# An mLSTM cell followed by a multiplicative FFN: first feed-forward pieces of one 128-token block each, with sums, copies and row transfers moved between engines

## The chip, the core and the metric

The kernel runs on one core of a Trainium2 chip. A core has TensorE (PE: matmuls; its weight loads are shown apart as PEld), VectorE (DVE), ScalarE (ACT) and GpSimd (POOL), and SyncE (SP), which here only issues DMAs; a few more are issued from ScalarE's queue. Each engine works through its own queue in order. The metric is the device time of one execution in microseconds (us), lower is better.

## The reference

Four batches (B), eight heads (H), 768 positions (S), head dimension 40 (D). The first half is a recurrence with a matrix state; its output is the input of a feed-forward network without nonlinearity:

```python
for t in range(S):
    m_new = maximum(f[:, :, t] + m, i[:, :, t])
    f_stab, i_stab = exp(f[:, :, t] + m - m_new), exp(i[:, :, t] - m_new)
    C = f_stab * C + i_stab * outer(v_t, k_t);   n = f_stab * n + i_stab * k_t;   m = m_new
    y[:, :, t] = sigmoid(o_t) * (C @ q_t) / maximum(abs(n . q_t), 1.0)
x = y.transpose(0, 2, 1, 3).reshape(B * S, H * D)          # 3072 x 320
a, b = x @ w1, x @ w2                                      # 320 x 1024 each
out = ((a * b) @ w3) @ w_out                               # w3 1024 x 1024, w_out 1024 x 320
```

All inputs and the output are float32.

## The kernel before

**Blocks and steps.** The sequence is cut into blocks of 128 tokens of one batch: `NU = 24` blocks, block n being part n // 4 of batch n % 4. Four blocks form a group of 512 tokens (`gr`) for the feed-forward part. The main loop runs over 32 steps `s`; step s computes the scores and states of block s, the outputs of block s-1, and some feed-forward work on earlier blocks. The order on TensorE is the order of the program text. For the other engines too, the text's order is kept (`keep_order`), so an instruction that waits holds up all that stand behind it on its engine. PSUM outside the cell's own banks is a pool of four banks (`ps_m`); pt, px, pa, pb, wp are tiles of it.

**The cell.** For each block k, q, v and the output gate o are loaded (`load`, `load_o`), k and q are turned so that head dimensions lie on partitions, by TensorE and ScalarE (`turn`, tile pt) for blocks below 10 (`N_DVE`). From block 10 on `load_turned` brings them with eight DMAs in 32-row strips and VectorE transposes them (L317); the second strip of each pair is shifted by 32 columns. `weights` takes exponentials on ScalarE (L303, tile pw), `masks` zeroes the upper triangle on GpSimd (L308). Scores (ss) and state updates (pc) go to the PSUM tile `cell[0]`, a block's own products (ph) and the earlier state's (pi) to `cell[1]` (`quarter_work`; for blocks 0 and 1 ph is a tile of its own). `outputs` makes h = pi * g + ph on VectorE: one product (L423) and four sums of a quarter each (L430). Its steps then take the absolute value of the normaliser (L438), the maximum (L440), the reciprocal (L441), multiply it with the gate (L443) and give y (L445). The column of ones behind v, set by a memset, is what yields the normaliser.

**Turning y.** For blocks below 15 (`NY`), `x_trans` turns y on TensorE (tile px) and ScalarE copies it to xT (L486); `twice` copies the last 64 columns a second time on GpSimd (L476). From block 15 on, `send` writes y to DRAM with four DMAs (L456, L458), `get_back` reads it with four (L465) and `x_turn` transposes on VectorE (L472).

**Weights.** The matrices are fetched as pairs of 32-bit words, piece by piece, in the order of the list `todo`: ten pieces of w1 and w2 (`w12`: first the five of columns 0 to 511, then the five of columns 512 to 1023; the last of each five is the remainder `wr`), eight of w_out (`wo`), sixteen of w3. `fetch` issues the DMA; `scale_next` scales both words on ScalarE (L191, L195); `convert` shifts one (L199) and adds the other (L200) on VectorE, which gives a float32 piece; pieces of w3 are also transposed there (L248). `n_cvt[s]` says how many pieces are converted at the end of step s, and `n_fetch` and `converted + 4` how far the fetches run ahead. w3 @ w_out is formed once (`w3_mm`, tile wp, kept as w3o), from step 9 on.

**Feed-forward.** `up(gr, fs, cs)` multiplies w1 and w2 columns of the groups `fs` (128 columns each) with the tokens `cs` (tiles pa, pb), `up_rest` adds the last 64 rows (`wr`, four quarters of the array at a time), copies pa on ScalarE (L638) and multiplies with pb on VectorE (L639, tile ab). The list `ups` holds pieces of two column groups for 256 tokens; steps 2 to 5 take one each, steps 6 to 15 two. From step 16 on follow the output products (`ffn_out`) and, for the last three groups, a scheme with seven products instead of eight (`up_by_seven`, `out_by_seven`).

**Around step 2.** `quarter_work(2)` computes the outputs of block 1 and then calls `between`, which turns y of blocks 0 and 1, converts weight pieces, and starts the first piece of `ups` for tokens 0 to 255. Between the two turns it runs filler on TensorE whose result nobody reads: `warm(1, small=38)`, one 128x512 product and 38 of 64x64.

## Time and profile before

| | |
|---|---|
| median of 3 runs | 427.33 us (426.63 to 430.44) |
| span of the profiled execution | 425.8 us; the page names no other time for this execution |
| busy: PE, DVE, POOL, ACT | 414.1, 313.5, 154.3, 150.1 us |
| mean granted TensorE clock | 0.996 |
| DMA | 51.15 MB, 135211 packets, 109360 of them under 512 B |

How to read it: busy time is the time in which an engine had an instruction in work; the ends of matmuls are modelled, so a busy TensorE isn't one at its peak. A float32 matmul shows as two records. "Lxx" is a line of the kernel; most matmuls are recorded on one helper line, L92, and are told apart by their tiles. In the chain of waits each row has its start in the span, its length, and the engine and tile; "SPq" is a DMA being issued on SyncE's queue, "issue" is time for which the profile shows no cause. In groups of instructions the columns are output and inputs, shapes, count, busy us and mean ns, and the idle time just before them.

### The profile page before, as it was taken

How to read it: one execution, taken by the hardware profiler on the slowest of the kernel's cores; microseconds unless marked ns; L12 is line 12 of the kernel's file. 1: busy time of each engine (PE TensorE's matmuls, PEld its weight loads, DVE VectorE, ACT ScalarE, POOL GpSimd, SP SyncE). 2: the span in 40 equal slices, each digit the busy share in tenths (PEclk: the TensorE clock that was granted, in tenths of full speed). 3: DMA queues.
4: the chain of work that ended last, by engine and by line, in shares of the span. 5: the costliest groups of instructions: out<-in, count | busy, mean ns of one | idle time of the engine just before them, and what ended most of it. 6: DMA issues, size and time to landing. Idle time of an engine off the chain costs nothing.

```text
span 425.8 us, 13079 instructions
## 1 busy us (share of the span) xinstructions
PE 414.1 (97%) x5353; PEld 335.3 (79%) x5353; DVE 313.5 (74%) x635; ACT 150.1 (35%) x404; POOL 154.3 (36%) x211
## 2 busy tenths in 40 slices
PE   7989989999999999999999999999999999999996
PEld 4768878888688788787777778788778879888896
DVE  6676986888949779778736966596868699575971
ACT  4766865567723623630433313032311110210000
POOL 4421342233303303303307751546453587542100
PEclk9989999999999999999999999999999999999999
DMA  8999998598977776985425675756421120000001
GB/s 186 204 173 245 214 144 140 134 193 180 215 183 154 166 182 135 181 164 105 89 80 130 153 141 121 142 133 117 87 44 36 35 39 2 31 2 31 2 32 62
DMA packets 135211, 51.15 MB, mean 120 GB/s; under 512 B 109360, under 2 KB 126960, under 8 KB 135152
## 3 DMA queue, kind: packets, MB, share of 16 engines
q1 hardware_dynamic: 131552, 46.29, 53.9%
q10 hardware_dynamic: 3600, 4.03, 2.7%
q8 instruction: 42, 0.69, 0.7%
q14 instruction: 17, 0.14, 0.1%
HBM read 44.50 MB, written 5.80 MB: 118 GB/s over the span
## 4 chain that ended last, share of the span: by engine, by line
PE 53%; issue 20%; DVE 7%; POOL 7%; SPq 7%; DMA 5%; ACT 1%; POOLq 0%; DVEq 0%
PE cell L92 17%; PE pa L92 12%; PE o L92 8%; PE pb L92 8%; PE p L92 3%; POOL pw L308 3%; SPq L184 3%; DVE w3T L666 2%; PE pt L95 1%; POOL vw L330 1%; SPq L148 1%; DMA raw<-in_moe_w_dram 1%; PE fill L92 1%; POOL raw L659 1%; POOL state L335 1%
## 5 line engine op out<-in xcount | busy, mean ns | idle before, releaser
L335 POOL TENSOR_TENSOR state<-state,decay 128x164 f32<-128x164 f32 x40 | 20.0, 500 | 154.8 <-DVE state L404 129.0
L92 PE MATMUL pa<-xT,w 128*128 128x256 f32 x240 | 60.4, 382 | 0.0
L92 PEld LDWEIGHTS pa<-xT,w 128*128 128x128 f32 x240 | 44.4, 190 | 6.8 <-DVE h L430 0.4
L303 ACT ACTIVATE pw<-pw,aT 128x64 f32<-128x64 f32 x184 | 46.4, 339 | 3.2 <-ACT o_sb L741 1.9
L92 PE MATMUL pb<-xT,w 128*128 128x256 f32 x192 | 45.4, 379 | 0.0
L729 POOL TENSOR_TENSOR ab<-ab,a_sb 128x512 f32<-128x512 f32 x22 | 29.4, 1356 | 32.2 <-DVE ab L684 32.2
L92 PEld LDWEIGHTS pb<-xT,w 128*128 128x128 f32 x192 | 36.4, 190 | 5.0
L711 POOL TENSOR_TENSOR wo<-wo 128x512 f32<-128x512 f32 x22 | 27.4, 1268 | 29.8 <-DVE wo L686 29.8
L92 PE MATMUL pa<-xT,wr 64*64 64x256 f32 x384 | 37.0, 386 | 0.5 <-DVE wr L200 0.5
L92 PE MATMUL wp<-wo,w3T 128*128 128x320 f32 x128 | 35.9, 433 | 1.1 <-DVE ab L639 0.6
L308 POOL TENSOR_SCALAR_AFFINE_SELECT pw<-pw 64x512 f32<-64x512 f32 x48 | 35.8, 746 | 3.0 <-ACT pw L303 1.2
L92 PE MATMUL pb<-xT,wr 64*64 64x256 f32 x384 | 36.4, 380 | 0.0
L92 PE MATMUL cell<-w3o,ab 128*128 128x320 f32 x128 | 35.4, 432 | 0.0
L638 ACT ACTIVATE a_sb<-pa 128x512 f32<-128x512 f32 x24 | 14.3, 598 | 59.0 <-PE pb L92 59.0
L639 DVE TENSOR_TENSOR ab<-pb,a_sb 128x512 f32<-128x512 f32 x24 | 16.4, 688 | 23.2 <-ACT a_sb L638 22.8
L92 PEld LDWEIGHTS wp<-wo,w3T 128*128 128x128 f32 x128 | 23.8, 190 | 10.5 <-DVE ab L639 0.8
L92 PEld LDWEIGHTS cell<-w3o,ab 128*128 128x128 f32 x128 | 24.3, 190 | 9.5
L92 PEld LDWEIGHTS pa<-xT,wr 64*64 64x64 f32 x384 | 18.9, 132 | 15.4 <-issue 8.8
L686 DVE SCALAR_TENSOR_TENSOR a_sb<-pa,wo 128x512 f32<-128x512 f32 x12 | 8.3, 689 | 29.8 <-PE pa L92 29.8
L430 DVE TENSOR_TENSOR h<-cell,h 64x164 f32<-64x164 f32 x88 | 28.6, 326 | 1.6
L92 PE MATMUL po<-w3o,ab 128*128 128x320 f32 x96 | 26.4, 433 | 0.0
L92 PEld LDWEIGHTS po<-w3o,ab 128*128 128x128 f32 x96 | 18.1, 190 | 7.3
(180 smaller groups left out, 846.4 us busy)
## 6 DMA issues: line engine op xcount, KB each, us to landing
raw<-in_moe_w_dram SPq DMA_DIRECT2D x64, 128.0 KB, 3.4
kbuf<-in_k_dram SPq DMA_DIRECT2D x24, 160.0 KB, 4.5
v_all<-in_v_dram SPq DMA_DIRECT2D x24, 160.0 KB, 4.9
o_in<-in_o_gate_dram SPq DMA_DIRECT2D x24, 160.0 KB, 4.8
pw<-U_d SPq DMA_DIRECT2D x28, 128.0 KB, 3.5
raw<-in_moe_w_dram SPq DMA_DIRECT2D x5, 512.0 KB, 6.7
raw<-in_moe_w_out_dram SPq DMA_DIRECT2D x8, 320.0 KB, 4.1
gates<-in_k_dram SPq DMA_DIRECT2D x28, 80.0 KB, 2.5
```

The costliest lines, as they stand in the source:

```text
L92: in_order(nc.tensor.matmul(out, lhsT=lhsT, rhs=rhs, start=start, stop=stop))
L184: nc.sync.dma_start(out=dst, in_=src)
L303: nc.scalar.activation(out=pw[:, h, :], in_=src[:, h, :], func=AF.Exp, bias=aT[:, c, b * H + h:b * H + h + 1])
L308: nc.gpsimd.affine_select(out=pw[r], in_=pw[r], compare_op=OP.is_ge, fill=0.0, base=0, pattern=[[0, H], [1, L]], channel_multiplier=-1)
L335: nc.gpsimd.tensor_tensor(out=new, in0=old, op=OP.mult, in1=decay[:, b * NP:(b + 1) * NP, 2 * c + x:2 * c + x + 1] .to_broadcast([P, NP, D1]))
L430: nc.vector.tensor_tensor(out=part, in0=ph[x][halves[e]], in1=part, op=OP.add)
L638: nc.scalar.mul(out=a_sb, in_=pa, mul=UP ** -2)
L639: nc.vector.tensor_tensor(out=ab_t[gr][j][:, fs[0]:fs[-1] + 1, t0:t0 + a_sb.shape[-1]], in0=pb, in1=a_sb, op=OP.mult)
L666: nc.vector.tensor_tensor(out=dst, in0=p, in1=q, op=OP.subtract)
L686: nc.vector.scalar_tensor_tensor(out=out, in0=p, scalar=UP ** -2, in1=q, op0=OP.mult, op1=OP.add)
L711: aside_by.tensor_tensor(out=kept[j][:, 1:4:2], in0=kept[j][:, 1:3], in1=kept[j][:, 3:4].to_broadcast([128, 2, TH]), op=OP.add)
L729: aside_by.tensor_tensor(out=t[:, f:FO:FH, :], in0=t[:, f:FO:FH, :], in1=a, op=OP.mult)
```

## The change

It has five parts.

- Group 0: the first four entries of `ups` are now one block (128 tokens) by four column groups (columns 0 to 511) each, for steps 2 to 5; the other half of group 0's columns follows in steps 6 and 7, in pieces as before. In step 2 the piece needs y of block 0 alone and is started as soon as that is turned; the outputs of block 1 are computed after it, and the filler is gone. In steps 4 and 5 the piece stands at the end of the step, behind the turn of the block it needs. The second five pieces of w1 and w2 are fetched and converted later (`n_cvt`, `n_fetch`): conversions are done by the end of step 5 instead of step 3.
- From block 10 on (`N_OWN`) ScalarE copies the four quarters of ph to SBUF, and VectorE adds them in one operation. For all blocks the normaliser is made in another order (the memset gives 2 instead of 1; reciprocal first, then the larger of it and its negative, then the smaller of that and 0.5).
- The sums of the eight `wo` pieces go to GpSimd instead of VectorE.
- k and q from block 10 on are loaded once (four DMAs instead of eight), and ScalarE copies the eight columns that the second strip needs (`shift`). A memset on GpSimd in step 4 clears the rest of that memory.
- y of blocks from 15 on is written to DRAM as whole rows (two DMAs instead of four) and read in pieces of 32 columns; the transposes write every fourth column instead of neighbouring ones.

```diff
-    def warm(n, m=4, small=0):
+    def warm(n, m=4):
         bank = mps([P, 4, P], "fill")
         for _ in range(n):
             mm(bank[:, 0:m], ident, ident.unsqueeze(1).to_broadcast([P, m, P]))
-        for i in range(small):
-            r = halves[i % 2]
-            mm(bank[r, 0, 0:L], ident[r, 0:L], ident[r, 0:L])
 
...
-    N_DIAG = 2
+    N_DIAG, N_OWN = 2, 10
...
-                for j in range(2):
-                    p0, c0 = hip * DP + j * 32, (1 - j) * 32
-                    nc.sync.dma_start(out=dst[p0:p0 + 32, c0:c0 + NP * RAW].rearrange("r (p e) -> r p e", p=NP),
-                                      in_=of.rearrange("p (r f) d -> r p (f d)", f=4))
+                nc.sync.dma_start(out=dst[hip * DP:hip * DP + 32, 32:TB].rearrange("r (p e) -> r p e", p=NP),
+                                  in_=of.rearrange("p (r f) d -> r p (f d)", f=4))
+
+    def shift(n):
+
+        for mem in turned_in[n % 2]:
+            e = mem[:, 32:TB].rearrange("r (g d) -> r g d", d=D)
+            for p0 in (0, DP):
+                nc.scalar.copy(out=e[p0 + 32:p0 + 64, :, 0:D - 32], in_=e[p0:p0 + 32, :, 32:D])
...
-    def to_f32(dst, raw):
-        bits, V = dst.bitcast(U32), nc.vector
-        V.tensor_scalar(out=bits, in0=raw[:, :, 1], scalar1=3, scalar2=None, op0=OP.logical_shift_left)
-        V.tensor_tensor(out=bits, in0=bits, in1=raw[:, :, 0], op=OP.add)
+    def to_f32(dst, raw, adder):
+        bits = dst.bitcast(U32)
+        nc.vector.tensor_scalar(out=bits, in0=raw[:, :, 1], scalar1=3, scalar2=None, op0=OP.logical_shift_left)
+        adder.tensor_tensor(out=bits, in0=bits, in1=raw[:, :, 0], op=OP.add)
...
-            to_f32(dst, raw)
+            to_f32(dst, raw, nc.gpsimd if dst.shape[-1] == DM else nc.vector)
             return
         w3 = wst.tile([128, CW], FP, name="w3", tag="w3")
-        to_f32(w3, raw)
+        to_f32(w3, raw, nc.vector)
...
+        if between:
+            between(lambda: outputs(s - 1, pi, ph))
+        elif 0 <= s - 1 < NU:
             den = outputs(s - 1, pi, ph)
             den()
-            if between:
-                for _ in range(3):
-                    den()
-                den = None
-                between()
-            if late:
...
-        nc.vector.tensor_tensor(out=h.rearrange("p (n two) d -> p two n d", two=2), in0=pi,
+        y = y_t[n] = sb.tile([P, DM + REM], FP, name="y", tag="y")
+        before = y[:, 0:H * D1].rearrange("p (h d) -> p h d", d=D1) if n >= N_OWN else h
+        nc.vector.tensor_tensor(out=before.rearrange("p (n two) d -> p two n d", two=2), in0=pi,
                                 in1=gT[:, c, hs].rearrange("p (n two) -> p two n", two=2).unsqueeze(3)
                                 .to_broadcast([P, 2, NP, D1]), op=OP.mult)
         if n < N_DIAG:
             nc.vector.tensor_tensor(out=h, in0=ph, in1=h, op=OP.add)
-        for x, e in quarters if n >= N_DIAG else ():
+        if n >= N_OWN:
+            for x, e in quarters:
+                nc.scalar.copy(out=h[halves[x], 0:H // 2] if x == e else h[halves[x], H // 2:H], in_=ph[x][halves[e]])
+        for x, e in quarters if N_DIAG <= n < N_OWN else ():
             part = h[halves[x], 0:H // 2] if x == e else h[halves[x], H // 2:H]
             nc.vector.tensor_tensor(out=part, in0=ph[x][halves[e]], in1=part, op=OP.add)
 
...
-            yield V.tensor_scalar(out=den.bitcast(U32), in0=h[:, :, D:D1].bitcast(U32), scalar1=0x7FFFFFFF, scalar2=None,
-                            op0=OP.bitwise_and)
-            yield V.tensor_scalar(out=den, in0=den, scalar1=1.0, scalar2=2.0, op0=OP.max, op1=OP.mult)
-            yield V.reciprocal(out=den, in_=den)
-            e = o_t.pop(n)
-            nc.vector.scalar_tensor_tensor(out=e, in0=e, scalar=1.0, in1=den.to_broadcast([P, H, D]), op0=OP.add, op1=OP.mult)
-            y_t[n] = sb.tile([P, DM + REM], FP, name="y", tag="y")
-            yield nc.vector.tensor_tensor(out=y_t[n][:, 0:DM].rearrange("p (h d) -> p h d", d=D), in0=h[:, :, 0:D],
-                                           in1=e, op=OP.mult)
+            if n >= N_OWN:
+                yield
+                V.tensor_tensor(out=h, in0=before, in1=h, op=OP.add)
+                V.reciprocal(out=den, in_=h[:, :, D:D1])
+            else:
+                yield V.reciprocal(out=den, in_=h[:, :, D:D1])
+            yield V.scalar_tensor_tensor(out=den, in0=den, scalar=-1.0, in1=den, op0=OP.mult, op1=OP.max)
+            v = h[:, :, 0:D]
+            yield V.scalar_tensor_tensor(out=v, in0=den.to_broadcast([P, H, D]), scalar=0.5, in1=v, op0=OP.min, op1=OP.mult)
+            yield V.scalar_tensor_tensor(out=y[:, 0:DM].rearrange("p (h d) -> p h d", d=D), in0=o_t.pop(n), scalar=1.0,
+                                         in1=v, op0=OP.add, op1=OP.mult)
...
-        for cc in range(KF):
-            nc.sync.dma_start(out=y_d[n][:, :, cc, :], in_=y[:, cc * P:(cc + 1) * P].rearrange("t (i c) -> t i c", c=32))
-        for i in range(0, 4, 2):
-            nc.sync.dma_start(out=y_d[n][:, i:i + 2, KF, :], in_=y[:, KF * P:DM].rearrange("t (i c) -> t i c", c=32))
+        nc.sync.dma_start(out=y_d[n][:, 0:DM], in_=y[:, 0:DM])
+        nc.sync.dma_start(out=y_d[n][:, DM:DM + REM], in_=y[:, KF * P:DM])
 
     back_t = {}
 
     def get_back(n):
         back_t[n] = sb.tile([P, 4, KC, 32], FP, name="yb", tag="yb", bufs=1)
         for i in range(4):
-            nc.sync.dma_start(out=back_t[n][32 * i:32 * (i + 1)].rearrange("r m k c -> r m (k c)"),
-                              in_=y_d[n][:, i].rearrange("(m r) k c -> r m (k c)", r=32))
+            nc.sync.dma_start(out=back_t[n][32 * i:32 * (i + 1)],
+                              in_=y_d[n].rearrange("(r m) (k i c) -> i r m k c", r=32, k=KC, i=4)[i])
...
-        nc.vector.transpose(out=x_t[gr][:, :, j * P:(j + 1) * P].rearrange("c k (m r) -> c k m r", r=32),
+        nc.vector.transpose(out=x_t[gr][:, :, j * P:(j + 1) * P].rearrange("c k (r m) -> c k m r", r=32),
...
-        nc.gpsimd.memset(vbuf[i][:, :, D:D1], 1.0)
+        nc.gpsimd.memset(vbuf[i][:, :, D:D1], 2.0)
...
-    nc.gpsimd.memset(gates[RG:P, NP * RAW:TB], 0.0)
...
-    ups = [(gr, [f, f + 1], slice(j * 2 * P, (j + 1) * 2 * P)) for gr in range(3) for j in range(2)
-           for f in range(0, FO, 2)]
+    ups = [(0, list(range(FO // 2)), slice(j * P, (j + 1) * P)) for j in range(GT)]
+    ups += [(gr, [f, f + 1], slice(j * 2 * P, (j + 1) * 2 * P)) for gr in range(3) for j in range(2)
+            for f in range(0 if gr else FO // 2, FO, 2)]
...
-    n_cvt = [0, 0, 2, 0, 1, 2, 3, 3, 3] + [2] * 6
-    n_fetch = [5, 5, 10]
+    n_cvt = [0, 0, 0, 1, 2, 2, 3, 3, 4, 3, 3] + [2] * 4
+    n_fetch = [5, 5, 7]
...
-                for _ in range(3):
-                    fetch(*todo.pop(0))
+                fetch(*todo.pop(0))
             load(s + 2, slice(0, 2))
             if s == 1:
                 load_o(2)
             if s == 2:
-                for _ in range(2):
-                    fetch(*todo.pop(0))
-                fetched = 10
+                fetch(*todo.pop(0))
+                fetched = 7
             load(s + 2, slice(2, 3))
...
-        open_ups = [up(*x) for x in now] if s != 2 else []
+        open_ups = [up(*x) for x in now] if s not in (2, 4, 5) else []
...
-            if s == 3:
-                scale_next()
-                scale_next()
-
-        def between():
+
+        def between(out):
+            x_trans(0)
+            for _ in range(2):
+                convert()
+            block = up(*now[0])
+            scale_next()
+            convert()
+            weights(2)
+            den = out()
+            for _ in range(4):
+                den()
+            weighted(2)
+            masks(2)
+            up_rest(*block)
+            turn(2)
             twice(1)
-            weighted(2)
+            x_trans(1)
             rows_of_u(3)
-            for _ in range(3):
-                scale_next()
-            for n in range(2):
-                x_trans(n)
-                if n == 0:
-                    warm(1, small=38)
-            for _ in range(3):
-                convert()
-            turn(2)
-            block = up(*now[0])
             weighted(3)
             weights(3)
             masks(3)
             out_gate(2)
-            convert()
-            up_rest(*block)
 
         gated = None
         if s <= NU:
-            gated = quarter_work(s, rest, between if s == 2 else None, convert if s == 3 else None)
+            gated = quarter_work(s, rest, between if s == 2 else None)
...
+                shift(s + 1)
...
-            turned, converted = 2, converted + (4 if s == 2 else 2)
+            turned, converted = 2, converted + (3 if s == 2 else 0)
...
+        late_ups = [up(*x) for x in now] if s in (4, 5) else []
         if s < NU:
-            if 0 < s < NU - 1 and s != 2:
-                if s != 1:
-                    weighted(s + 1)
+            if s == 1:
+                for _ in range(2):
+                    scale_next()
+            elif 0 < s < NU - 1 and s != 2:
...
+            nc.gpsimd.memset(gates[RG:P, 0:5 * TC], 0.0)
...
+        for x in late_ups:
+            up_rest(*x)
```

More of the change, by code (lines that the diff above doesn't have):

```diff
@@ L127 @@
     KC = KF + 1
-    y_d = [dram.tile([P, 4, KC, 32], FP, name=f"y_d{n}") if n >= NY else None for n in range(NU)]
+    y_d = [dram.tile([P, KC * P], FP, name=f"y_d{n}") if n >= NY else None for n in range(NU)]
     o_t, u_t = {}, {}
@@ L336, in decayed, with quarter_work @@
                                 .to_broadcast([P, NP, D1]))
-    def quarter_work(s, rest, between, late):
+    def quarter_work(s, rest, between):
         rest()
@@ L367, in quarter_work @@
         den = None
-        if 0 <= s - 1 < NU:
+        if between:
+            between(lambda: outputs(s - 1, pi, ph))
+        elif 0 <= s - 1 < NU:
             den = outputs(s - 1, pi, ph)
             den()
-            if between:
-                for _ in range(3):
-                    den()
-                den = None
-                between()
-            if late:
-                late()
         n, first_read = s, None
@@ L408, in quarter_work @@
                     decayed(after, second, n, 1)
-            if late:
-                late()
             if den:
@@ L951 @@
                 turn(s + 1)
+        late_ups = [up(*x) for x in now] if s in (4, 5) else []
         if s < NU:
-            if 0 < s < NU - 1 and s != 2:
-                if s != 1:
-                    weighted(s + 1)
+            if s == 1:
+                for _ in range(2):
+                    scale_next()
+            elif 0 < s < NU - 1 and s != 2:
+                weighted(s + 1)
                 weights(s + 1)
```

## The prediction

> **What bounds the kernel now.** I read the page first: busy shares, then the clock row; then the waits of TensorE, the chain of waits of the early microseconds, a table by stretches, and the groups by form.
>
> ```profile
> PE 414.1 (97%) x5353; PEld 335.3 (79%) x5353; DVE 313.5 (74%) x635; ACT 150.1 (35%) x404; POOL 154.3 (36%) x211
> ```
> TensorE has 11.7 us without work in 425.8. Only what shortens its own queue, or fills those 11.7, can show. Its waits before 60 us (total, times, longest):
>
> ```profile
> PE cell L92 <- issue: 1.9, 2, 1.5
> PE fill L92 <- POOL ident masks.py:199: 1.6, 1, 1.6
> PE px L95 <- DVE y L445: 1.2, 1, 1.2
> PE pa L92 <- DVE wr L200: 0.5, 1, 0.5
> ```
> After 60 us the same view has 2.0 us in all. So the change is decided before 60 us, where TensorE's queue also holds filler (chain of waits: start, length, what):
>
> ```profile
> 21.20 0.87 DVE o_in L443
> 22.09 0.83 DVE y L445
> 22.96 0.83 PE px L95 x3
> 23.79 4.69 PE fill L92 x78
> 28.48 0.48 PE px L95 x3
> 28.96 0.87 PE pt L95 x8
> 29.83 1.73 PE pa L92 x8
> 31.56 1.73 PE pb L92 x8
> ```
> Step 2 turns y of block 0 (px), runs filler until block 1's y is there, turns that, and only then starts the first feed-forward piece (pa, pb), since it covers both blocks' 256 tokens. The table by stretches (length; busy us and instructions of PE, PEld, DVE, ACT, POOL; granted clock; DMA share; GB/s):
>
> ```profile
> 20.00:23.40 3.40, 2.21 (x52) 1.74 (x52) 2.79 (x8) 2.37 (x8) 2.14 (x4) 1.00 1.22 165
> 23.40:26.80 3.40, 3.40 (x30) 1.90 (x31) 3.02 (x9) 2.79 (x6) 0.50 (x2) 0.50 0.96 146
> 48.00:60.00 12.00, 10.52 (x297) 9.26 (x290) 11.03 (x27) 6.72 (x21) 5.07 (x10) 1.00 0.89 193
> 60.00:107.00 47.00, 46.70 (x798) 40.00 (x800) 37.25 (x82) 30.71 (x82) 13.36 (x24) 1.00 0.84 166
> ```
> The filler ran at half clock for 3.4 us; from 48 to 60 us VectorE (11.03 of 12) is the tight engine; from 60 us TensorE is full.
>
> **The change, part by part.**
>
> *First four blocks, step 2.* Gone: the filler, 4.69 us. The piece for block 0 alone (4 column groups, 128 tokens) multiplies as much: 16 passes of 128 columns replace 8 of 256, for each of pa and pb. Eight passes of 256 took 1.73 us, 216 ns each. For 128 columns the nearest rows are the pt transposes, each with a weight load of its own: 8 in 0.87 us, 109 ns; the 160-column passes of L92 (o) took 1.09 us for 8, 136 ns. Both go by columns, so I take 108 ns and no change. The upper bound is a weight load that nothing hides, 190 ns.
>
> VectorE's end of step 1 gets shorter: L443 and L445 took 0.87 and 0.83 beside GpSimd's mask of block 2, and 0.49 each at 24.6 us without it. That mask now comes later, so y(0) ends at 21.8, not 22.9. px starts at 21.85; its copy on ScalarE is queued behind the tanh of o(1), whose data landed at 22.02, so pa starts near 23.1. It needs w2 and wr: wr's second half was issued at 18.0 and was scaled at 24.6 without a wait, so its sum is there near 25.9, before pb is through. At full clock: 23.1 + 3.46 (pa, pb) + 1.02 (wr part, as at 33.3) = 27.6; pt 0.87; block 1's y, now after three conversions on VectorE (25.7 + 2.6 = 28.3) and GpSimd's mask and copy (28.9); px; a copy of kT and qT; scores and state 0.78: the next piece starts at 30.3 instead of 35.09. If the half clock stays, 1.7 us of work is lost and it starts at 32.0.
>
> The row on the clock: the stretch from 20.0 to 23.4 with 2.21 us of work was followed by 3.4 us at 0.50, filler or not. The new order adds perhaps 0.4 us of work there. [...] No stretch after 26.8 falls under 0.87 busy in the table, so I keep the one loss in half of the cases.
>
> *Second halves of w1 and w2 two steps later; steps 3 to 6.* Before, from 35.09 to the end of step 6's wr parts at 69.55: 34.5 us, of which the conversions cost 0.5 (L200) and the unexplained issue wait 1.5. Each step of TensorE: piece 3.46, wr 1.0, pt 0.87, px 0.48, cells 1.7, 7.5 in all. VectorE per step after: ab 0.6, h 0.5, four sums 1.4, pw 0.6, den and reciprocal 0.3, states 0.5, two products 1.1, rows of U 0.7 (twice in step 4), and 1.1 per conversion, of which steps 3, 4, 5 have 1, 2, 2: 6.8, 8.5 and 8.0. So VectorE sets the pace twice. First: step 4 has no piece at its start, so TensorE is done with pt(4) 1.4 us before the weighted scores are ready, and the state adds 0.5. Second: step 6's pb needs the conversion that ends step 5's queue: 0.9. Together 2.8 against the 2.0 before. DMA is no bound: three of ten pieces are asked for a step later and needed two steps later. Sum at step 6, without the half clock: 4.8 - 0.8 = 4.0; with it: 3.1 - 0.8 + 0.5 = 2.8 (VectorE, which sets the pace there, does not lose the clock's time: I give back 0.5). Middle 3.4.
>
> *w_out's sums on GpSimd.* Eight sums leave VectorE (L200, 0.62 each: 5.0 us over steps 6 to 8). GpSimd's integer sum is not in the trace; nearest is vw, 128x328 f32, 0.76; bounds 0.57 (VectorE) and 2.0 (128x640, contended). I take 0.8. Behind them wait the next step's state product and vw: 2.4 + 3.4 of 11.9 us a step.
>
> *Later conversions.* Steps 8, 9, 10 have 4, 3, 3 instead of 3, 2, 2. One of w3 costs 0.4 + 0.7 + 1.1 = 2.25 us. Step 9: 8.2 + 6.75 = 15 us of VectorE against 11.9 of TensorE, so the next ab comes up to 3 us late and holds back a PSUM bank that TensorE wants. That took 0.6 us in step 9 now (PE wp waits for ab). Bounds 0 and 3; I take 1.
>
> *Own outputs by ScalarE, from block 10.*
>
> ```profile
> L430 DVE TENSOR_TENSOR h<-cell,h 64x164 f32<-64x164 f32 x88 | 28.6, 326 | 1.6
> L404 DVE TENSOR_TENSOR state<-cell,state 128x164 f32<-128x164 f32 x20 | 6.4, 321 | 0.0
> ```
> Four sums of 0.33 become one of 128x328 (0.5 to 0.8) on VectorE and four copies on ScalarE (0.21 for the smallest row, 0.43 for 128x320; 0.3 taken). Also four shifting copies, same bounds: 2.4 us a step on an engine busy 35%. Behind the shifts wait the exponentials and tanh of the next block; the loads they wait for are issued a step ahead, as those that VectorE's transposes never waited for (0.0). The absolute value goes too, and two small steps merge. VectorE is then 1.2 us a step sooner from step 11, where TensorE does not wait for it, except 0.4 (w3T, 242.8) and 0.2 (o, 356.1): +0.5. Halved loads k, q: four issues less a step, 1.7 us of SP, not on the path.
>
> *Rows once.* L456 and L458 become one whole-row write and one small one; L465 reads 128-byte pieces. The round trip now is 3.78 + 1.95 us, and y(23) has 3.3 us to spare (349.05 to 352.4). The transposes write every fourth word: 0.57 to 0.9 by the ratio of L317 (1.10) to L295 (0.70). Hidden by that spare; without it 0.3 to 2 us once. The memset 32x1280 on GpSimd (0.3 to 1.7 us) is hidden by its idle share.
>
> **Sum.** 3.4 (4.0 or 2.8), +0.5 late, -0.4 (1.0 for the late conversions, of which 0.6 is paid already), and of the 1.9 us of issue waits, which sit where DMA is fullest, I take 0.8 as gone (bounds 0 and 1.5): 4.3. Span 425.8 - 4.3 = 421.5; the median of the runs, 427.33, lies 1.5 above this span, so 423.0.
>
> **Rivals.** (A) The forecast: 421 to 425, centre 423.0. (B) More: no half clock (4.8 in step 2), VectorE's two waits overlap (2.0, as now), the long issue wait does not return (1.5), late 0.5: 6.8, so 420.5. For: these waits stand alone in the trace, with nothing queued that would bring them back. Against: 2.2 us of 3.4 was too thin a stretch for the clock. (C) VectorE takes the place: half clock (2.8), issue waits stay, 3 us lost in steps 9 and 10 (2.4 more than now), late 0.5: 0.9, so 426.4. For: 11.03 of 12 at 48 to 60 us. Against: the sums that leave it for GpSimd. (D) Slower: weight loads bound the four 128-token pieces. Place: pa and pb of steps 2 to 5, 4 x 32 = 128 passes. Price at 190 ns: 128 x 82 ns = 10.5 us, so 433.5. It eats the gain of 4.3 from 142 ns a pass (108 + 34) and is slower by over 1% from 175. For: that is PEld's mean for such a load. Against: 109 ns for pt, with a load each.
>
> **How the numbers follow.** A 0.50, B 0.22, C 0.18, D 0.10, with any other queue that loses as much. About 1% (4.3 us, so 423.1 is the border) is what a measurement of this kernel can tell. A lies across it, 0.27 of its 0.50 below: faster 0.27 + 0.22 = 0.49; same 0.23 + 0.18 = 0.41; slower 0.10. The range takes A, B but for its end, and C with 2 us for the loads not foreseen: 419.0 to 428.5.
>
> **What would show it.** Right: no filler between the px of blocks 0 and 1; pa starting near 23; 16 passes in 1.73 us; step 6's pieces starting near 56; TensorE full from there. The clock row tells the half clock. Wrong if TensorE waits more than 3 us for VectorE in steps 4 to 6 or 9 to 11, if a 128-column pass takes over 120 ns, or if ScalarE waits for k and q loads.

## The result, and the profile after

The changed kernel takes 441.44 us (median of 4 runs, 439.6 to 442.75) against 426.98 of the kernel before (4 runs, 425.67 to 430.44): ratio 1.034, 95% interval 1.028 to 1.040. The forecast was 423.0, with 428.5 as the end of its range. So the change costs 14.5 us. The profiled execution took 442.08 us, with a span of 440.4 (before: 425.8). Of all runs below one, of the filler in step 4, took 438.11 us where the other eleven of its kernel took 428.85 to 431.96; it is left out of the comparisons.

The page after, its busy line and its clock row:

```profile
PE 419.0 (95%) x5403; PEld 340.6 (77%) x5403; DVE 297.7 (68%) x561; ACT 181.8 (41%) x516; POOL 165.3 (38%) x219
...
PEclk9998989999789999999999999999999999999999
```

VectorE lost 15.8 us of work and ScalarE gained 31.7, as the change intends. TensorE's busy time rose from 414.1 to 419.0 although 4.7 us of filler are gone, and its time without work from 11.7 to 21.4. The clock row has three dents where before had one. The waits of TensorE (total, times, longest):

```profile
PE pa L92 <- ACT xT L486: 7.4, 3, 3.9
PE px L95 <- issue: 3.4, 2, 2.6
PE cell L92 <- ACT wo L701: 1.9, 5, 0.4
...
PE cell L92 <- issue: 1.3, 1, 1.3
```

Only the last was in the view of before, with 1.9 us. Two name ScalarE, the engine that the prediction took to have room to spare. The stretches (length; busy us and instructions of PE, PEld, DVE, ACT, POOL; granted clock; DMA share; GB/s) show what follows a wait:

```profile
38.04:41.45 3.41, 1.78 (x68) 1.48 (x66) 2.99 (x10) 3.41 (x12) 1.33 (x2) 1.00 1.07 137
41.45:44.87 3.42, 3.42 (x70) 3.34 (x60) 3.24 (x7) 1.93 (x4) 2.34 (x4) 0.50 0.94 184
48.00:60.00 12.00, 9.38 (x203) 9.01 (x202) 9.95 (x22) 7.44 (x20) 6.02 (x11) 0.86 1.04 166
51.69:55.11 3.42, 0.80 (x7) 0.67 (x8) 3.20 (x8) 0.13 (x1) 0.48 (x1) 1.00 0.91 125
55.11:58.53 3.42, 3.42 (x19) 3.42 (x18) 3.04 (x8) 3.01 (x10) 1.57 (x3) 0.50 0.84 219
60.00:107.00 47.00, 47.00 (x756) 40.13 (x757) 30.28 (x61) 26.51 (x68) 18.26 (x28) 1.00 0.69 143
113.13:116.55 3.42, 0.55 (x3) 0.03 (x1) 3.18 (x5) 1.93 (x5) 2.79 (x6) 1.00 0.85 179
116.55:119.96 3.41, 2.38 (x6) 1.93 (x7) 3.15 (x5) 1.31 (x4) 0.25 (x1) 0.50 1.02 167
119.96:123.38 3.42, 3.42 (x10) 2.70 (x9) 2.92 (x4) 0.00 (x0) 0.00 (x0) 0.50 0.88 242
```

Stretches with 1.78, 0.80 and 0.55 us of matmuls are each followed by one at half clock; behind the last it lasts two stretches, 116.55 to 123.38. A full stretch at half clock (0.50 for 3.41 us) loses 1.7 us of work.

**Where the 14.5 us sit.** The start of the products of pw and v in `cell` marks every step on TensorE. Taken from the timelines, it gives this table: how many us later than in the profile of before each step begins there (a minus is earlier). Every row is one execution, while the times below are medians, each compared with runs of the kernel before taken beside it. The profile of before is itself a rather long execution: its span is 425.8 us, and the median span of 35 later runs of the same kernel is 424.2. So a lead of 1 to 2 us in the table is no gain. "Step 9" below means from that mark of step 9 to that of step 10. Between steps 9 and 12 one must know that a product wp (4.5 us) of step 9 moved to step 11 with the later conversions.

```
                              step 3     6     9    10    12    14    18    24
changed kernel                 -5.0   1.5   1.0   3.5   7.1  11.2  11.2  14.4
xT copy first                  -3.3   0.5   0.5  -4.1  -0.5   0.4   0.3   3.6
no shifts, eight loads         -5.1  -1.5  -1.6   2.1   5.7   8.7   8.7   8.8
late parts only                -1.3  -1.9  -2.3  -2.2   0.2   5.1   5.1   8.3
early part only                -2.8   1.4   1.7   4.4   8.0   9.2   9.2   9.2
xT first, nothing on ScalarE    1.6   7.9   7.8   3.9   7.5   8.7   8.7   8.5
xT first, own sums on VectorE  -4.3   2.5   2.0  -2.6   1.0   1.6   1.6   1.4
split pieces                   -4.1   4.1   3.7   3.8   3.1   3.1   3.1   3.0
split pieces, ScalarE's work   -1.6   4.9   4.4   4.5   3.8   3.8   3.8   7.2
relief                         -2.4  -1.4  -1.9  -1.1  -0.9  -0.9  -0.9  -1.1
relief, shorter filler         -4.1  -3.6  -3.5  -2.7  -3.4  -3.4  -3.4  -3.1
before with a dose on ScalarE  -2.8  -2.4  -1.4  -1.5  -0.1   1.9   1.9   2.1
```

The first row has three losses: 6.5 us from step 3 to step 6, which eat the 5.0 won in step 2; 10.1 from step 9 to step 14; and 3.2 from step 18 to step 23, 0.65 in each of five steps.

*The gain in step 2.* The chain of waits after (start, length, what) is the forecast's:

```profile
21.00 0.77 PE px L95 x3
21.79 0.49 ACT xT L486
22.33 2.05 PE pa L92 x16
24.38 1.79 PE pb L92 x16
...
29.96 1.98 PE pa L92 x16
```

No filler; pa at 22.33 (forecast 23.1); the next piece at 29.96 (forecast 30.3, before 35.09). The 16 passes of 128 columns take 112 to 117 ns each, by their spacing (pb from 24.38 on, 1.79 us for 16).

*The loss in step 9.* First before, then after (start, length, engine, line, operation, shapes, count, idle time before and what ended it):

```profile
108.35 8.88 PE L92 MATMUL wp<-wo,w3T 128*128 128x320 f32 x32 [0.58 <-DVE ab L639]
116.22 0.46 ACT L486 COPY xT<-px 128x384 f32<-128x384 f32 x1
```

```profile
109.10 4.58 PE L92 MATMUL wp<-wo,w3T 128*128 128x320 f32 x16 [0.29 <-DVE ab L638]
117.04 0.49 ACT L486 COPY xT<-px 128x384 f32<-128x384 f32 x1
117.58 3.78 PE L92 MATMUL pa<-xT,w 128*128 128x256 f32 x8 [3.91 <-ACT xT L486]
```

The copy to xT comes within a microsecond of where it came before. What is missing is the second product wp, which had kept TensorE at work until the copy was there.

*The loss in step 13.* ScalarE's queue after, and then TensorE's (start, length, engine, line, operation, shapes, count, idle time before and what ended it):

```profile
182.44 1.19 ACT L427 COPY h<-cell 64x164 f32<-64x164 f32 x4 [1.16 <-DVE y L420]
183.66 1.25 ACT L151 COPY gates<-gates 32x128 f32<-32x128 f32 x4
184.94 2.02 ACT L305 ACTIVATE pw<-pw,aT 128x64 f32<-128x64 f32 x8
...
189.45 0.46 ACT L486 COPY xT<-px 128x384 f32<-128x384 f32 x1
```

```profile
182.60 4.47 PE L92 MATMUL wp<-wo,w3T 128*128 128x320 f32 x16
189.96 1.99 PE L92 MATMUL pa<-xT,w 128*128 128x256 f32 x8 [2.89 <-ACT xT L486]
```

And the queues of ScalarE and TensorE in a step of before with the same work:

```profile
173.13 2.01 ACT L303 ACTIVATE pw<-pw,aT 128x64 f32<-128x64 f32 x8
...
177.64 0.46 ACT L486 COPY xT<-px 128x384 f32<-128x384 f32 x1
```

```profile
174.61 4.47 PE L92 MATMUL wp<-wo,w3T 128*128 128x320 f32 x16
178.92 1.89 PE L92 MATMUL pa<-xT,w 128*128 128x256 f32 x8
```

In both, TensorE turns y (px), runs wp for 4.5 us and then needs xT. In both, ScalarE's copy to xT stands at the end of its queue for the step: exponentials, tanh, four scalings, then xT. Before, the exponentials started as soon as the piece was copied, xT was ready at 178.1 and TensorE needed it at 178.9: the cover (work of TensorE that goes on while the copy is made) was enough by 0.8 us. After, the copies of h stand first. They wait 1.16 us for VectorE's product of the cells (L420), take 1.19, the shifts take 1.25, and xT is ready at 189.9 when wp ended at 187.1.

*The loss in steps 18 to 22* is the same queue with another customer, the copies of partial products to wo (L703, L701), which must free PSUM before TensorE goes on:

```profile
273.43 1.19 ACT L427 COPY h<-cell 64x164 f32<-64x164 f32 x4 [3.03 <-DVE y L420]
...
278.69 0.57 ACT L701 COPY wo<-cell 128x512 f32<-128x512 f32 x1
```

```profile
279.31 8.88 PE L92 MATMUL cell<-w3o,ab 128*128 128x320 f32 x32 [0.34 <-ACT wo L701]
```

Before, ScalarE had been idle there and waited for TensorE:

```profile
265.52 0.60 ACT L704 ACTIVATE wo<-cell 128x512 f32<-128x512 f32 x1 [4.04 <-PE cell L92]
```

From the mark of step 19 to these products it takes 8.50 us now and took 7.97 before, of which the wait is 0.34; in all a step is 0.65 us longer.

### The profile page after: what moved, and what is told of

Its sections match the earlier page's. It is cut to its first block, busy times and chain, and to the rows that moved or that the text cites. A ratio compares the mean times of both kernels' runs of the same rounds, so it can differ in the third digit from the quotient of the medians.

```text
span 440.4 us, 13164 instructions
## 1 busy us (share of the span) xinstructions
PE 419.0 (95%) x5403; PEld 340.6 (77%) x5403; DVE 297.7 (68%) x561; ACT 181.8 (41%) x516; POOL 165.3 (38%) x219
## 4 chain that ended last, share of the span: by engine, by line
PE 72%; ACT 10%; DVE 6%; SPq 4%; DMA 4%; issue 3%; POOL 0%; DVEq 0%; ACTq 0%; POOLq 0%
PE pa L92 18%; PE cell L92 15%; PE pb L92 12%; PE o L92 8%; PE po L92 6%; PE wp L92 6%; PE p L92 3%; ACT pw L305 3%; SPq L136 2%; ACT h L427 2%; DMA w3o<-in_moe_w_dram 2%; PE px L95 2%; DVE ab L683 1%; PE pt L95 1%; DVE pw L769 1%
## 5 line engine op out<-in xcount | busy, mean ns | idle before, releaser
L337 POOL TENSOR_TENSOR state<-state,decay 128x164 f32<-128x164 f32 x40 | 23.7, 594 | 155.8 <-DVE state L401 128.7
L92 PE MATMUL pa<-xT,w 128*128 128x256 f32 (+1 forms) x272 | 63.9, 372 | 7.4 <-ACT xT L486 7.4
L92 PEld LDWEIGHTS pa<-xT,w 128*128 128x128 f32 x272 | 48.2, 201 | 14.7 <-ACT xT L486 8.8
L92 PE MATMUL pb<-xT,w 128*128 128x256 f32 (+1 forms) x224 | 46.7, 355 | 0.0
L92 PEld LDWEIGHTS pb<-xT,w 128*128 128x128 f32 x224 | 38.8, 195 | 4.6
L310 POOL TENSOR_SCALAR_AFFINE_SELECT pw<-pw 64x512 f32<-64x512 f32 x48 | 31.9, 666 | 15.8 <-ACT pw L305 14.3
L92 PE MATMUL pa<-xT,wr 64*64 64x256 f32 (+1 forms) x416 | 37.0, 369 | 0.0
L92 PE MATMUL pb<-xT,wr 64*64 64x256 f32 (+1 forms) x416 | 36.4, 363 | 0.0
L427 ACT COPY h<-cell 64x164 f32<-64x164 f32 x56 | 16.2, 290 | 33.1 <-DVE y L420 29.8
L92 PEld LDWEIGHTS pb<-xT,wr 64*64 64x64 f32 x416 | 21.6, 133 | 3.0
```

Source lines behind the costliest of these rows:

```text
L92: in_order(nc.tensor.matmul(out, lhsT=lhsT, rhs=rhs, start=start, stop=stop))
L310: nc.gpsimd.affine_select(out=pw[r], in_=pw[r], compare_op=OP.is_ge, fill=0.0, base=0, pattern=[[0, H], [1, L]], channel_multiplier=-1)
L337: nc.gpsimd.tensor_tensor(out=new, in0=old, op=OP.mult, in1=decay[:, b * NP:(b + 1) * NP, 2 * c + x:2 * c + x + 1] .to_broadcast([P, NP, D1]))
L427: nc.scalar.copy(out=h[halves[x], 0:H // 2] if x == e else h[halves[x], H // 2:H], in_=ph[x][halves[e]])
```

## The experiments

The theory (Q): TensorE lost its time to ScalarE's in-order queue, in which copies that wait for the cells' results (by the trace for VectorE's product of them, L420) now stand ahead of copies that TensorE waits for; with step 9 it was open whether those copies, the weights or the missing wp decide. The rival (V): VectorE's longer list of conversions sets steps 9 to 13.

### The xT copy first

```diff
+        while s + 1 >= N_DVE and turned < min(s - 1, NY):
+            x_trans(turned)
+            turned += 1
         with tc.issue_after(gated.ins) if gated else nullcontext():
             if seven:
                 seven[3]()
```

> The changed kernel with one edit: from step 9 on, the transposes and the copy of y into xT (px, xT) are written right behind the cells of the step before, so that ScalarE's copy to xT stands ahead of the shifts, the exponentials and the scaling of raw weights instead of behind them; TensorE's order stays. Theory Q (ScalarE's queue: TensorE waits in steps 9 and 13 for an xT copy that stands behind ScalarE's new copies and the raw weights; an idle stretch then costs half clock): the waits of 3.9 and 2.9 us for xT and the half clock at 116.7 to 123.5 us (3.4 us lost) go, the lateness of 0.65 us in each of the five steps 18 to 22 stays, so 441.4 - 9 = about 432. Theory V (VectorE's longer list of conversions sets steps 9 to 13, the xT copy only stands beside it): under 2 us, 439.5 to 441.5, and TensorE waits for ab or for weights instead.

431.79 us (429.82 to 432.54), ratio 1.012 (1.007 to 1.016). TensorE's queue is the same, only the text order of one ScalarE copy changed, and 9.6 us are back. In the table the loss from step 9 to step 14 is gone (0.5 to 0.4), and that of the late steps is whole (0.3 to 3.6). Theory V falls: the list of conversions was the same and the loss went.

### No shifts

`load_turned` with its eight transfers as before, `shift` and the memset of step 4 taken out.

> The changed kernel, with k and q of the later blocks loaded by eight transfers a step as before, so that no shifting copies stand on ScalarE; all else as changed. Theory Q: 1.25 us of ScalarE's queue a step go. The five late steps get back their 0.65 us each (3.2 us), the wait of step 13 falls from 2.9 to 1.6; that of step 9 falls from 3.9 to 2.6 if the queue decides it, and stays if the landing of the raw weights (115.9 us) does. Together 4.5 to 6 us: 435.5 to 437. Theory V: same as changed, 440 to 442, or slower by SyncE's four more issues a step.

440.43 us (436.47 to 441.98; ratio 1.031, 1.025 to 1.038), outside what Q expected and inside the 440 to 442 of V. The run before speaks against V. In the profile, taken of the fastest of the four runs, two of Q's three terms hold. The late steps lose nothing (8.7 to 8.8). Step 13's wait is 1.6 us. But step 9's wait is 6.3 us and not 2.6 or 3.9. The copy to xT came at 116.78 there and at 117.04 in the changed kernel: at the same time, whatever ScalarE had to do before, because it stands behind scalings of raw weights that had not landed (four waits for them between 107 and 116 us, the longest 2.9). TensorE was 2.7 us earlier in this run, so it waited longer. Before waited 3.0 us for such landings in the same place. So in step 9 the shifts decide little: the copy comes when the weights have landed, and there is no second wp to cover that. The median lies 4 us above the profiled run, and where the other runs lose them no profile shows.

### Late parts only, early part only

The change's parts taken apart: the kernel before with ScalarE's copies and shifts, rows once, w_out's sums and the division (`late parts only`), and the kernel before with the order of the first blocks and the schedule of conversions (`early part only`).

> The kernel before with only the later parts of the change: own outputs copied by ScalarE, halved loads with shifts, rows once, sums of w_out on GpSimd and the shorter division; the first six steps and the schedule of conversions as before. If the cover is what step 9 lost (two products wp stood between px and the next piece in that step before, one after, 4.5 us each), then no wait for xT in step 9 and no half clock there; step 13 keeps about 2.9 us with 0.7 before it, the late steps 3.2: 427 + 6.5 = 433.5. If ScalarE's new copies alone make the loss of steps 9 to 14: 427 + 13 = 440. If the early steps alone make the loss: 427.

> The kernel before with only the first part of the change: first four blocks for 128 tokens by four column groups, second half of w1 and w2 two steps later with the conversions that this moves; loads of k and q, own outputs, rows and w_out's sums as before. By the lateness of the changed kernel at step 6 (1.5 us) and with one product wp as cover in step 9 (wait for xT of 2.5 to 4 us, half clock behind it 1.7 to 3.4): 427 + 6 to 8.5, about 434. If ScalarE's new copies make the loss: 427 + 1.5 = 428.5. If the early part saves what was forecast: 424.

436.77 us (436.02 to 438.93; ratio 1.025, 1.020 to 1.030) and 436.18 (434.43 to 440.01; 1.023, 1.015 to 1.031). Added, 10.3 + 9.7 is more than the change's 14.5.

With the late parts alone, step 9 loses nothing (-2.3 to -2.2), since two products wp stand there again; then two waits for xT come, of 1.9 and 2.9 us, with one stretch at half clock, and the 3.2 us of the late steps. With the early part alone there is one wait of 5.5 us in step 9 with a half clock behind it, and nothing later. So the two parts spoil different steps in the same way. Both runs lie 2 to 3 us above what I expected. In the profiles I had counted one wait in steps 11 to 14 where there were two, and up to 4 us in step 9 where there were 5.5.

### Own sums on VectorE, and nothing on ScalarE

Both with the xT copy first. One has `N_OWN = NU`, so that VectorE adds the own outputs; the other has that and the eight loads.

> As the run with the xT copy first, and own outputs added by VectorE again, with the shifts left on ScalarE. The late steps lost 0.65 us each by the sum of what stands ahead of the copy to wo on ScalarE (four copies of h behind the cells, four shifts). Without the shifts the loss was 0; theory Q says that without the copies of h it is 0 as well, since they hold 1.2 us and a wait for the cells: 428.5. If only the shifts cost: 431.8.

> The changed kernel with the xT copy written behind the cells (as in the run before that did this alone), and ScalarE without its new work: own outputs added by VectorE, k and q loaded by eight transfers. What is left of the change: the early part, the schedule of conversions, rows once, w_out's sums on GpSimd, the shorter division. Theory Q: no wait for xT in steps 9 to 14 and no 0.65 us in steps 18 to 22: 431.8 - 3.3 = 428.5, that is before + 1 to 2, which is the early part's own. If the late steps are slow for another cause (GpSimd, rows), 431.5.

429.38 us (427.18 to 431.56; 1.008, 1.006 to 1.011) and 433.07 (431.83 to 436.0; 1.017, 1.012 to 1.022). The late steps cost nothing in either (1.6 to 1.4, 8.7 to 8.5), and nothing without the shifts alone, so it is the sum on the queue that counts. The 0.8% that the first still loses stands before step 6 in the table (2.5 us), in the early part. The second missed its number by 4.6 us. In its profile 7.9 us were lost by step 6, with five stretches at half clock and 5.0 us of cell waits for which the profile shows no cause; its loads differ only from step 8 on. Its other runs (431.83 to 433.19) are all slower than those of the first kernel too. Ahead of step 8 the two kernels differ only in where GpSimd clears a part of memory (at the start, or in step 4), and the cause is left open.

### A dose on ScalarE

The kernel before, with ScalarE's new load but not its waits:

```diff
+    idle_mem = const.tile([P, H // 2, D1], FP, name="idle_mem")
...
+        if n >= 10:
+            for x, e in quarters:
+                nc.scalar.copy(out=idle_mem[halves[x]], in_=idle_mem[halves[x]])
+            for x, e in quarters:
+                r = idle_mem[32 * x:32 * x + 32].rearrange("p h d -> p (h d)")[:, 0:128]
+                nc.scalar.copy(out=r, in_=r)
```

> The kernel before, with eight copies on ScalarE in each step from 11 on that have the shapes of the new ones (four of 64x164, four of 32x128, 2.45 us) but work on a memory of their own and wait for nothing. It tells ScalarE's load from the place of its waits. Theory: in steps 11 to 14 the copy to xT comes 2.45 us later, of which 0.7 to 1.6 us are spare: 0.8 and 1.7 us lost; in steps 18 to 22 nothing is lost, since ScalarE was idle 4 us ahead of the copy to wo and the new copies cost there only through their wait for the cells: 426 + 2.5 = 428.5. If load alone counts, 0.65 us more in each of five steps: 431.8.

429.91 us (428.29 to 433.8; 1.008, 1.005 to 1.011). Its waits of TensorE:

```profile
PE pa L92 <- ACT xT L494: 2.6, 2, 1.8
```

That is 0.8 and 1.8, as expected (0.8 and 1.7), and the late steps lose 0.2 us in all instead of 3.2. The median lies 1.4 us above the 428.5 expected. So in steps 11 to 14 load alone is enough to break the cover. In steps 18 to 22 it isn't: there the same copies cost only where they wait (for L420, 3.03 us in the row above) and hold back what stands behind them. Why they wait for VectorE's product, which reads the same tile `cell` but writes nothing that they read, is open.

### Split pieces

Could the 5 us of step 2 be kept? Here blocks 0 and 1 get 128-token pieces in steps 2 and 3, and steps 4 and 5 the other four column groups for both, at the step's start; the conversions are as early as before. Once without ScalarE's new work, once with it, both with the xT copy first.

```diff
-    ups = [(0, list(range(FO // 2)), slice(j * P, (j + 1) * P)) for j in range(GT)]
+    ups = [(0, list(range(FO // 2)), slice(j * P, (j + 1) * P)) for j in range(2)]
...
-    n_cvt = [0, 0, 0, 1, 2, 2, 3, 3, 4, 3, 3] + [2] * 4
-    n_fetch = [5, 5, 7]
+    n_cvt = [0, 0, 2, 3, 1, 2, 3, 3, 3] + [2] * 6
+    n_fetch = [5, 5, 10]
```

> The kernel without ScalarE's new work, and with a part of the early change alone: blocks 0 and 1 for 128 tokens by four column groups in steps 2 and 3, then both blocks for the other four column groups in steps 4 and 5 at the step's start, blocks 2 and 3 from step 6 as before; second half of w1 and w2 and all conversions at the times of the kernel before. Theory: the 5 us won in step 2 (3.3 with half clock) were lost in steps 4 to 6, where no piece stood at the step's start and TensorE waited for VectorE (1.3 us) and fell to half clock; with the pieces back at the start at least 3 us stay: 427 - 3.5 = 423.5, range 421.5 to 425. Rival: VectorE, with five more conversions in steps 2 and 3, holds those steps back by as much: 427.

> The same early part and schedule, with ScalarE's new work (copies of h, shifts, halved loads) and the xT copy first. Theory Q: 3.3 us above the run without that work, all in steps 18 to 22: 426.5 to 427; two products wp stand in step 9 again, which the xT copy no longer needs.

430.33 us (429.15 to 430.51; 1.009, 1.006 to 1.013) and 431.66 (429.84 to 434.89; 1.011, 1.007 to 1.016). The first expectation missed by 6.8 us:

```profile
PE pb L92 <- DVE w L204: 3.9, 2, 3.6
```

```profile
42.94 0.66 ACT L195 ACTIVATE raw<-raw 128x512 f32<-128x512 f32 x1
44.53 0.69 DVE L204 CUSTOM_DVE_ANT_0 w<-raw,w 128x1024 uint16<-128x1024 uint16 x1
45.37 0.73 PE L92 MATMUL pb<-xT,w 128*128 128x256 f32 x2 [3.56 <-DVE w L204]
```

TensorE reached the second column half 3 us sooner than in before and stood there until VectorE had converted it; a half clock followed, from 45.85 us on (-4.1 at step 3, 4.1 at step 6). The piece that it waited for was scaled at 42.94 without a wait for its landing, and its conversion stood behind VectorE's work on the cells of step 3; only the last piece, the remainder, waited 0.4 us for its landing. In before the conversions came at about the same time, just as TensorE needed them. The rival named was right: VectorE. With ScalarE's work the late 3.3 us are back (3.8 to 7.2); in the medians 1.3 us show, with runs 5 us apart, so the times alone do not tell the two kernels apart.

### Filler where TensorE waits in step 4

One filler matmul of 512 columns ahead of step 4's cells, on the kernel with own sums on VectorE.

> The run with the xT copy first and own outputs on VectorE (429.4), with one filler matmul of 512 columns (0.9 us) put where TensorE waits 1.33 us for VectorE at the start of step 4. If a window of 3.41 us with little work brings the half clock, the one behind 38 to 41 us goes where it was: 0 to 1.7 us less, mean granted clock from 0.991 towards 0.996, 428.5. If filler in that place does nothing for the clock: 429.4 to 430.

430.47 us (428.85 to 431.96; 1.009, 1.006 to 1.011) against 429.38 without (1.008, 1.006 to 1.011). The mean granted clock was 0.9915 over the eleven runs, as over the ten without. The filler did nothing for the clock; whether it cost its time these intervals don't tell. In the two profiles the half clock isn't behind step 4 at all, but at 53.3 to 60.1 us without the filler and at 53.9 to 60.7 with it.

### Relief alone, a shorter filler, and the transpose behind the conversions

The kernel before with only rows once, w_out's sums on GpSimd and the shorter division; then with `warm(1, small=14)` instead of 38; then also with `rows_of_u(3)` behind the three conversions of step 2.

> The kernel before with only what takes work from VectorE or the queues and puts none on ScalarE: w_out's sums on GpSimd, rows once, the shorter division; first steps, loads of k and q, own outputs as before. In the run with all later parts on the early part of before, TensorE was 1.9 to 2.3 us ahead of before up to step 11, and what was lost came behind it from ScalarE's copies. Theory: without these the lead stays, 426 - 1.5 = 424.5, range 423 to 426. If that lead was chance (1.2 us of it was a shorter issue wait near 58 us, which differs from run to run), 426.

> The same, with the filler between the transposes of blocks 0 and 1 cut from 76 to 28 small matmuls: 48 of 39 ns at half clock are 1.9 us, at full clock 0.9. y of block 1 is done before the filler ends, so TensorE would go on sooner, by 0.9 to 1.9 us: 423 to 424. Rival, from the run of the split pieces, where the lead of step 2 ended in a wait for weights: it is lost again by step 5, 424.5; or the thinner window brings a half clock more, 426.

> The run with the shortened filler, and in step 2 the transpose of block 3's rows of U (0.7 us of VectorE) behind the three conversions instead of ahead of them, since TensorE's pb waited 1.3 us and the wr parts 0.6 us for those. If a lead of step 2 stays when the pieces stand at the start of their steps and the weights are there: 0.7 us less, 424.4, and the lateness table keeps -4 from step 3 to the end. If every lead of step 2 ends in a wait for weights by step 6, as in the run with the split pieces: 425.1 as without, with the wait moved to steps 3 to 5.

426.23 us (424.93 to 430.6), 425.07 (424.31 to 429.26) and 425.38 (424.65 to 427.53). The ratios are 0.9991 (0.9963 to 1.0019), 0.9977 (0.9947 to 1.0007) and 0.9971 (0.9948 to 0.9995). The relief by itself is worth nothing that can be measured; its profile has much the same lead in the table as that of the late parts (-1.9 and -2.3 at step 9), about as much as the profile of before is longer than usual. With less filler, the lead of step 2 stays to the end in the one profile (-4.1, -3.6, -3.1), of which the medians show 1.15 us. The 39 ns at half clock that were expected for a small matmul of the filler are near the mean in the profile of before, 40 ns (76 of them in 3.05 us); by their spacing there it is 53 ns at half clock and 29 at full. With the transpose moved the interval lies just below 1, the only one here that does: 1.0 us less than before. Its own profile does not show where: it has 10.2 us at half clock from 19.8 us on, and an issue wait of 1.5 us. Between the last two, nothing can be told.

## Why the prediction was wrong, point by point

**Step 2: right, with some luck.** Filler gone, pa within 0.8 us, the next piece within 0.4, the pass at 112 to 117 ns for 108. Rival D, weight loads at 190 ns, is out. The half clock that was given half of the chances did not come in this execution. With the same first steps it did come in three others, from 22.84 us (xT copy first), 23.85 us (early part only) and 20.78 us on (nothing on ScalarE); there the table has -3.3, -2.8 and 1.6 at step 3 instead of -5.0.

**Steps 3 to 6: the mechanism was half right and the size wrong.** The net gain at step 6 was put at 3.4 us; the profile has a loss of 1.5. The six rows of the table with these first steps run from -1.5 to 7.9 there, so the loss differs much from one execution to the next. VectorE's wait at step 4 was priced at 1.4 and is 1.33 (the page calls it "issue"; it ends at 39.69, when VectorE's weighted scores are done at 39.6); the two smaller waits of that sum, 0.5 and 0.9, are not in the view. What was left out: two more stretches at half clock (41.5 and 55.1 us, 1.7 each); and an issue wait of 2.62 us at 52 us where before had 1.49. The term "1.9 us of issue waits, 0.8 taken as gone" has the wrong sign: 3.4 us now, 2.62 of them here. Of the 6.5 us lost from step 3 to step 6, the half clock makes 3.4, VectorE's wait 1.33, a wait for pw 0.30 and the longer issue wait 1.13; a wait of 0.51 that before had there is gone. That is 5.65, and 0.85 are not accounted for. These sizes are read from one profile, and no run took one of these causes away alone. "DMA is no bound" held: no wait of TensorE in steps 3 to 6 is put down to a load.

**The half clock: the table of before was too coarse.** I kept one loss in half of the cases, because no stretch after 26.8 us fell under 0.87 busy in the table of before. That is a statement about before, and about stretches of 12 us or more. In stretches of 3.41 us before had a thin one as well, behind which the clock stayed full:

```profile
57.55:60.96 3.41, 1.93 (x27) 1.83 (x26) 3.30 (x11) 1.03 (x3) 0.00 (x0) 1.00 0.60 127
```

Of the changed kernel's stretches with less than that, three (1.78, 0.80 and 0.55 us of matmuls) were followed by half clock and one (1.68, from 188.23 us) was not. So the half clock came three times and not once at most, and behind stretches that were thinned and not empty. Each stretch at half clock is 3.41 us or a multiple, and those of one run lie on one grid: 41.45, 55.11 and 116.55 are 4 and 18 periods apart.

**Later conversions: the term that failed in step 9.** It was priced at 1 us, for ab coming late on VectorE. VectorE was not it: TensorE waits 0.3 us for ab. Each conversion has a scaling on ScalarE and a transfer, and a schedule that is one step later leaves one wp instead of two between px and the piece that needs xT. In before, xT was ready at 116.7 us and the second wp ended at 117.2, a cover of half a microsecond that no view of waits shows, since nothing waited. Without that wp: 3.9 us of wait, and then pa and pb at half clock in 6.4 us instead of 3.46, 2.9 lost.

**Own outputs by ScalarE: the term with the wrong sign.** Priced as a gain of 0.5 us, "on an engine busy 35%". Measured: a wait of 2.9 us in step 13 and 3.2 in steps 18 to 22. The durations were right (copies 0.29 us, shifts 0.295). The prediction named what stands behind the shifts, exponentials and tanh, and asked only whether those have time. It did not go on to the last instructions in the queue, the copies to xT and to wo. It looked for waits for the loads of k and q; ScalarE waited for VectorE's product of the cells instead (L420), 29.8 us in all, ahead of the first copy.

**GpSimd's sums, rows once: right.** From the groups by form after:

```profile
L440 DVE TENSOR_TENSOR h<-y,h 128x328 f32<-128x328 f32 x14 | 7.9, 562 | 8.3 <-ACT h L427 8.3
L472 DVE STREAM_TRANSPOSE xT<-yb 128x384 f32<-128x384 f32 x9 | 8.1, 896 | 0.1
L202 POOL TENSOR_TENSOR wo<-wo,raw 128x320 uint32<-128x320 uint32 x8 | 7.1, 917 | 0.2
```

The sum takes 0.92 us (0.8 taken), the transposes 0.90 (0.9), the sum of h 0.56 (0.5 to 0.8). The last columns of the first line show the other side of the new copies: VectorE waits 8.3 us for them.

**The rivals.** None was this case. D was the slower one and had another cause; its 0.10 also held "any other queue that loses as much", which is what came, and which queue was not named. C, VectorE in the place of the waits removed, came nearest in steps 3 to 6 and was far too small. None of the three signs of being wrong came either: all three looked at VectorE, at the passes and at the loads of k and q, and none at the end of ScalarE's queue.

## What to carry to other kernels

An engine at 35% busy is not free: what counts is how long before its due time the last instruction of its queue is done that another engine waits for, and that slack stands in no view of waits. Before putting work on such an engine, list its queue for one step of each kind, mark the copies that TensorE needs, and compare their end with the end of what covers them (here 0.5 and 0.8 us); then write those copies ahead of anything new that waits. A later schedule of side work also moves the matmuls made from it, and those may be the cover of something else.

## What the runs showed of the hardware

**Issue waits, and packets of the queue called instruction.** In the fifteen profiles there are 21 waits called "issue" in the middle of a series of matmuls between 10 and 70 us, 0.2 to 3.7 us long (the 1.33 us at the start of step 4 are VectorE's and not counted). Three of them are in the profiles of before and of the changed kernel. Each of these ends 1.27 to 1.45 us after the end of a packet of 16,384 bytes on the DMA queue that the page calls "q8 instruction" (42 packets, 0.69 MB): in before packets ended at 16.95 and 57.69 and TensorE went on at 18.22 and 59.05, in the changed kernel the packet ended at 53.11 and TensorE went on at 54.56. In six of the kernels with the early part a wait falls at the same instruction, after the first of step 5's three px transposes. No run changed these packets; that TensorE waits for them is a reading of the times and was not shown. They come with busy and with idle DMA engines: the engines' share was 1.01 during the 2.62 us of the changed kernel, 0.33 during the 1.49 us of before, and 0.13 in the stretch of 3.42 us that holds one of 0.68 us (split pieces, ScalarE's work).

**How thin a stretch brings the half clock.** On the grids of the twelve profiles that have a half clock, taken up to 310 us, all ten stretches of 3.41 us at full clock with 1.56 us of matmuls or less were followed by half clock. From 1.68 to 2.64 us it went both ways: eleven were followed by it, others with as little (1.68, 1.73, 1.74) were not; behind 2.7 us or more it never came. Estimated from these ten, a wait of 2 us, which leaves 1.41 of 3.41, would be enough if it fell into one stretch; and where the grid lies differs from run to run (the first half clock began at 23.41 us in before and at 41.45 in the changed kernel, 5.3 periods apart).
